# Folding channels c and c + 128 after the token transform, with the value path kept apart in three blocks of four

## The chip, the cores and the metric

The kernel runs on one core of a Trainium2 chip. The metric is the device time of one execution in microseconds (us). Every execution told of here was granted TensorE clock 0.999 to 1.0. PE is the tensor engine, DVE the vector engine, ACT the scalar engine, POOL GpSimd.

Differences under about 1 us between two programs are not read from their times. They are read, where possible, from the traces of the steady part, whose durations repeat within 0.02 us from batch to batch, apart from one or two chunks that differ by 0.1 to 0.3.

## The reference, cut to what matters

```python
X = np.fft.fft(x, axis=1)           # x: 8 batches x 3008 tokens x 256 channels
X = np.fft.fft(X, axis=2).real      # the mixing
g, val = X @ w_gate, X @ w_val      # 256 -> 1536
out = (gelu(g) * val) @ w_out       # 1536 -> 256
```

## The kernel before: the parts that matter

The token transform is split in two stages, and the channel transform stands between them. Stage 1 multiplies x with constants G and gives `A`; the channel stage multiplies `A` with cosines and sines `CS` and gives `Z`; the E, B and O packs (64-column matmuls on `Z`) give the even and odd parts of the mixed signal for half of the tokens. The feed-forward part ("layer 1", "layer 2") then makes token t and its mirror T - t from E + O and E - O.

```python
# stage 1, per group of 4 j: 2 x 4 matmuls of N=96, two evacuations on ACT
for cc in range(2):                       # channels 0..127, 128..255
    ...
    nc.tensor.matmul(ps[:, jj*96:(jj+1)*96], xt[:, j0+jj, cc*128:(cc+1)*128], G[:, j0+jj, :], ...)
# s1_ev: copies ps (128x384) to A[:, cc, ...], bf16

# channel stage, per pair of k2: 4 matmuls of N=256, one evacuation on DVE
for d in range(2):
    for cc in range(2):
        nc.tensor.matmul(ps[:, d*C:(d+1)*C], A[:, cc, k2+d, :], CS[:, cc, :], start=(cc==0), stop=(cc==1))
nc.vector.tensor_copy(Z[k2, k2+1], ps)

# layer 1 works on blocks fc of 128 hidden units, 12 per chunk, 3 chunks (512, 512, 481 tokens) per batch
def apart(ci, fc):
    return fc % 6 != 5 and (b, ci) != (0, 0)
# apart:     5 matmuls (gate E, O, M; value E, M), three DVE operations, product on POOL
# not apart: 6 matmuls (gate E, O, M; value E, O, M), two DVE products straight from PSUM
```

Work on the next batch (stage 1, channel stage, E/B/O) is slotted as "filler" between the blocks of the current batch: a batch has 36 slots, one per block. Batch 0's own transform is a head before the first block, and batch 1's filler is squeezed into the last 24 slots of batch 0. The head also makes all constants.

## Time and profile before

690.7 us is the median (690.18 to 691.16).

| | PE | DVE | POOL | ACT |
|---|---|---|---|---|
| busy, share of the span | 96% | 87% | 74% | 66% |
| busy in batch 3, of 81.01 us | 81.01 | 73.48 | 63.97 | 54.70 |

A busy PE is not a PE at its peak, so the chain of waits is read as well. This is the first line of the chain part of the page of the kernel before (shares of the span by engine):

```profile
PE 93%; POOL 3%; DVE 1%; ACT 1%; issue 1%; POOLq 0%; DVEq 0%; ACTq 0%
```

And this is the chain view of the same kernel for 275 to 356 us, nearly one batch of the steady part (shares of that stretch by engine, tile and line):

```profile
by line: PE ps_o L595 38.9%; PE ps_g L502 28.3%; PE ps_v L502 20.4%; PE ps_dft L402 6.5%; PE ps_dft L365 3.4%; PE ps_dft L427 0.8%; PE ps_dft L452 0.8%; PE ps_dft L440 0.8%
```

In the steady part nothing but PE is on the chain. L402 is the channel stage: 6.5% of it. The price of a matmul is its spacing, not its duration (durations overlap). The timeline of PE gives it: four matmuls of N=256 start at 301.58 and the next group at 302.02, so 110 ns each; two of N=512 are 216 ns apart.

```profile
301.15 0.38 PE L502 MATMUL ps_v<-EO_sb,WvE 128*128 128x512 bf16 x1
301.37 0.38 PE L502 MATMUL ps_v<-EO_sb,WvM 128*128 128x512 bf16 x1
301.58 0.60 PE L402 MATMUL ps_dft<-CS,A_sb 128*128 128x256 bf16 x4
302.02 1.04 PE L595 MATMUL ps_o<-Wo_sb,h_sb 128*128 128x256 bf16 x8
```

Finally, the groups (line, engine, operation, out<-in and shapes, count, busy us and mean ns, idle before) of what the change touches:

```profile
L412 DVE CAST Z_sb<-ps_dft 128x512 bf16<-128x512 f32 x88 | 60.1, 683 | 1.3 <-PE ps_dft L402 1.3
L402 PE MATMUL ps_dft<-CS,A_sb 128*128 128x256 bf16 x372 | 56.8, 274 | 0.3 <-DVE EO_sb L456 0.3
L379 ACT ACTIVATE A_sb<-ps_dft 128x384 bf16<-128x384 f32 x115 | 50.9, 503 | 0.6 <-PE ps_dft L365 0.5
L236 DVE CAST x_sb<-x_plain 94x1024 bf16<-94x1024 f32 x5 | 3.5, 695 | 0.6 <-DMA x_plain<-in_x_dram 0.6
```

### The profile page before, as it was taken

The page shows a single profiled execution, that of the slowest core. Times are in us where ns is not written, and L with a number is a line of the kernel's source. Part 1 is how long each engine was busy: PE and PEld are TensorE (multiplying, and loading weights), DVE is VectorE, ACT ScalarE, POOL GpSimd, SP SyncE. Part 2 cuts the span into 40 slices and gives each one's busy share as a digit, 9 for nine tenths or more (in the row PEclk, how much of TensorE's full clock was granted, in tenths as well). Part 3 has the DMA queues.
Part 4 walks back from the last instruction along what each step waited for, and adds up shares of the span by engine and source line. Part 5 has one row for each costly group of instructions (what it writes and reads, how often), then busy time and mean ns, then how long its engine had stood idle before and what let it go on. Part 6 is the DMA issues. An engine that isn't in the chain of part 4 may idle for free.

```text
span 689.5 us, 14359 instructions
## 1 busy us (share of the span) xinstructions
PE 664.8 (96%) x5290; PEld 455.7 (66%) x5290; DVE 603.0 (87%) x969; ACT 452.1 (66%) x892; POOL 507.0 (74%) x288
## 2 busy tenths in 40 slices
PE   2899999999999999999999999999999999999995
PEld 2556677766667666666667667676676666666664
DVE  7698899899988999889998899889998899999980
ACT  5689667756676656866678556776668666666650
POOL 8305777877887887788778868877886787798980
PEclk9999999999999999999999999999999999999999
DMA  8970611251114321161112621211112121221122
GB/s 234 208 151 17 129 39 38 50 116 40 43 35 90 75 47 35 44 120 45 39 40 47 117 47 33 46 37 38 40 39 47 28 47 32 47 47 43 38 51 62
DMA packets 36278, 43.44 MB, mean 63 GB/s; under 512 B 6668, under 2 KB 33292, under 8 KB 34700
## 3 DMA queue, kind: packets, MB, share of 16 engines
q1 hardware_dynamic: 32432, 30.47, 18.6%
q0 software_dynamic: 3184, 11.57, 9.4%
q8 instruction: 41, 0.67, 0.4%
q10 hardware_dynamic: 592, 0.49, 0.3%
q14 instruction: 29, 0.24, 0.1%
HBM read 29.43 MB, written 24.64 MB: 78 GB/s over the span
## 4 chain that ended last, share of the span: by engine, by line
PE 93%; POOL 3%; DVE 1%; ACT 1%; issue 1%; POOLq 0%; DVEq 0%; ACTq 0%
PE ps_o L595 36%; PE ps_g L502 26%; PE ps_v L502 19%; PE ps_dft L402 6%; PE ps_dft L365 3%; POOL h_sb L572 1%; PE ps_dft L452 1%; PE ps_dft L427 1%; PE ps_dft L440 1%; PE ps_v L332 0%; PE ps_g L332 0%; POOLq L758 0%; DVE out_sb L608 0%; DVE A_sb L381 0%; PE ps_v L402 0%
## 5 line engine op out<-in xcount | busy, mean ns | idle before, releaser
L572 POOL TENSOR_TENSOR h_sb<-gelu_sb,v_sb 128x1024 bf16<-128x1024 bf16 (+1 forms) x230 | 481.4, 2107 | 155.0 <-ACT gelu_sb L560 66.3
L595 PE MATMUL ps_o<-Wo_sb,h_sb 128*128 128x256 bf16 (+1 forms) x2304 | 299.2, 272 | 3.9 <-DVE out_sb L608 2.2
L517 ACT ACTIVATE gelu_sb<-ps_g 128x512 bf16<-128x512 f32 (+1 forms) x288 | 169.0, 587 | 150.9 <-PE ps_g L502 150.5
L595 PEld LDWEIGHTS <-h_sb 128*128 128x128 bf16 (+1 forms) x2304 | 220.5, 100 | 44.2 <-issue 5.0
L535 DVE SCALAR_TENSOR_TENSOR ve_sb<-EB_sb,w_97,ps_v 128x512 f32<-128x512 bf16 (+1 forms) x230 | 167.6, 729 | 22.6 <-PE ps_v L502 19.7
L560 ACT ACTIVATE gelu_sb<-ps_g 128x512 bf16<-128x512 f32 (+1 forms) x288 | 168.0, 584 | 2.8 <-PE ps_g L502 2.8
L539 DVE SCALAR_TENSOR_TENSOR v_sb<-ps_v,ve_sb 128x512 f32<-128x512 f32 (+1 forms) x230 | 155.4, 675 | 16.5 <-POOL h_sb L572 0.6
L541 DVE SCALAR_TENSOR_TENSOR v_sb<-ps_v,ve_sb 128x512 f32<-128x512 f32 (+1 forms) x230 | 153.8, 669 | 0.0
L502 PE MATMUL ps_g<-EO_sb,WgM 128*128 128x512 bf16 (+1 forms) x288 | 108.3, 376 | 0.0
L502 PE MATMUL ps_g<-EO_sb,WgO 128*128 128x512 bf16 (+1 forms) x288 | 108.2, 376 | 0.0
L502 PE MATMUL ps_v<-EO_sb,WvE 128*128 128x512 bf16 (+1 forms) x288 | 108.0, 375 | 0.0
L502 PE MATMUL ps_g<-EO_sb,WgE 128*128 128x512 bf16 (+1 forms) x288 | 108.0, 375 | 0.0
L502 PE MATMUL ps_v<-EO_sb,WvM 128*128 128x512 bf16 (+1 forms) x288 | 104.4, 376 | 0.4 <-DVE h_sb L547 0.2
L615 ACT ACTIVATE out_sb<-ps_o 128x512 f32<-128x512 f32 x92 | 55.0, 598 | 37.6 <-PE ps_o L595 36.0
L412 DVE CAST Z_sb<-ps_dft 128x512 bf16<-128x512 f32 x88 | 60.1, 683 | 1.3 <-PE ps_dft L402 1.3
L402 PE MATMUL ps_dft<-CS,A_sb 128*128 128x256 bf16 x372 | 56.8, 274 | 0.3 <-DVE EO_sb L456 0.3
L402 PEld LDWEIGHTS <-A_sb 128*128 128x128 bf16 x384 | 38.1, 100 | 24.3 <-issue 1.2
L575 DVE TENSOR_TENSOR h_sb<-gelu_sb,ps_v 128x512 bf16<-128x512 bf16 (+1 forms) x58 | 39.2, 677 | 15.0 <-ACT gelu_sb L560 13.0
L379 ACT ACTIVATE A_sb<-ps_dft 128x384 bf16<-128x384 f32 x115 | 50.9, 503 | 0.6 <-PE ps_dft L365 0.5
L365 PEld LDWEIGHTS <-x_sb 94*128 94x128 bf16 x512 | 30.6, 102 | 29.7 <-DVE x_sb L236 14.4
L502 PEld LDWEIGHTS <-WvE 128*128 128x128 bf16 x288 | 28.2, 98 | 32.2
L502 PEld LDWEIGHTS <-WvM 128*128 128x128 bf16 x288 | 28.2, 98 | 30.8 <-issue 0.8
(101 smaller groups left out, 393.5 us busy)
## 6 DMA issues: line engine op xcount, KB each, us to landing
out_dram<-out_sb SPq DMA_DIRECT2D x361, 64.0 KB, 2.0
x_sb<-in_x_dram POOLq DMA_DIRECT2D x14, 752.0 KB, 7.8
x_plain<-in_x_dram SPq DMA_DIRECT2D x4, 384.0 KB, 7.6
x_plain<-in_x_dram SPq DMA_DIRECT2D x2, 768.0 KB, 8.1
Wo_sb<-in_moe_w_out_dram POOLq DMA_DIRECT2D x2, 384.0 KB, 6.0
wg_hi<-in_moe_w_gate_dram SPq DMA_DIRECT2D x2, 256.0 KB, 3.8
wv_hi<-in_moe_w_val_dram SPq DMA_DIRECT2D x2, 256.0 KB
wg_lo<-in_moe_w_gate_dram SPq DMA_DIRECT2D x2, 256.0 KB, 4.8
```

The costliest lines, as they stand in the source:

```text
L365: nc.tensor.matmul(ps[:, jj * 96 : (jj + 1) * 96], xt[:, j0 + jj, cc * 128 : (cc + 1) * 128], G[:, j0 + jj, :], start=True, stop=True,)
L402: nc.tensor.matmul(ps[:, d * C : (d + 1) * C], A[:, cc, k2 + d, :], CS[:, cc, :], start=(cc == 0), stop=(cc == 1),)
L412: nc.vector.tensor_copy(_sub(Z, [[1, 2 * C]], k2 * C), ps)
L502: nc.tensor.matmul(ps[:, :n], W[nm, part][:, fs], src, start=start, stop=stop, **kw)
L517: nc.scalar.activation(gl[:, 0, :n], pg[:, :n], AF.Gelu)
L535: nc.vector.scalar_tensor_tensor(ve[:, :n], EB_bufs[b][:, c0 : c0 + n], w128[:, fc : fc + 1], pv[:, :n], op0=ALU.mult, op1=ALU.add)
L539: nc.vector.scalar_tensor_tensor(vv[:, 0, :n], po[:, :n], -0.5, ve[:, :n], op0=ALU.mult, op1=ALU.add)
L541: nc.vector.scalar_tensor_tensor(_sub(vv, [[-1, n]], TOK + n - 1), po[:, :n], 0.5, ve[:, :n], op0=ALU.mult, op1=ALU.add)
L560: nc.scalar.activation(dst, pg[:, :n], AF.Gelu)
L572: nc.gpsimd.tensor_tensor(st["h"][:, fc, :, :n], gl[:, :, :n], pv[:, :, :n], op=ALU.mult)
L595: nc.tensor.matmul(pso[:m, sign, :], st["h"][:, fc, sign, h0 : h0 + m], Wo_sb[:, fc, :], start=(fc == 0), stop=(fc == NFC - 1),)
L615: nc.scalar.activation(osb[:m], pso[:m], AF.Copy)
```

## The change

For even output channels the cosine and sine of channel c + 128 equal those of c, for odd ones they are their negatives. So the sum of channels c and c + 128 is enough for the even outputs, and their difference for the odd ones. The intent is to form both once, when stage 1 is evacuated, and to halve the columns of the channel stage's matmuls. DVE pays for the folds; Z's and O's evacuations move from DVE to ACT, and a further block in each chunk takes the six-matmul form, which costs DVE less and PE more.

```diff
 # stage 1, batches 1..7
-                s1_ev(j0, "AA")
+                up = up_tile()
+                nc.scalar.activation(up8, hi, AF.Copy)
+                for g, op in enumerate((ALU.add, ALU.subtract)):
+                    nc.vector.tensor_tensor(dst, lo, up8, op=op)      # dst in A[:, g]
 ...
             work.append(s1_pack(j0))
+            work.append(lambda: None)                                 # folds in every second filler place
 # channel stage
-                    for cc in range(2):  matmul(ps[:, d*C:(d+1)*C], A[:, cc, k2+d, :], CS[:, cc, :], ...)
+                    for g in range(2):   matmul(ps[:, o:o+128], A[:, g, k2+d, :], CS[:, g, :], start=True, stop=True)
-                    nc.vector.tensor_copy(Z, ps)
+                    nc.scalar.activation(Z, ps interleaved, AF.Copy)  # batch 0 alternates ACT and DVE, as before
 # O pack
-                nc.vector.tensor_copy(EO, ps)
+                nc.scalar.activation(EO, ps, AF.Copy)
 # value
-            return fc % 6 != 5 and (b, ci) != (0, 0)
+            return fc % 4 != 3 and (b, ci) != (0, 0)
 # head: batch 0's x
-    def cast_x(j0, nj, on_act=False):  one copy fp32 -> bf16 (DVE; j0 = 20 on ACT)
+    def fold_x(j0, nj):                add and subtract of two fp32 halves -> bf16, all on DVE
 # also: smaller constants CS without a POOL product, output buffers 3 -> 2
```

More of the change, by code (lines that the diff above doesn't have):

```diff
@@ L86 @@
     TPI = const_pool.tile([128, 2 * K1], BF16)
-    CS = const_pool.tile([128, 2, C], BF16)
+    CS = const_pool.tile([128, 2, 128], BF16)
     W = {}
@@ L113, in gelu_tile, with up_tile @@
         return work_pool.tile([128, 2, TOK], BF16, tag="gelu", bufs=4, name="gelu_sb")
+    def up_tile():
+        return work_pool.tile([128, 384], FP32, tag="up", bufs=2, name="up_sb")
     def ve_tile():
@@ L121, in osb_tile @@
     def osb_tile():
-        return work_pool.tile([128, 2, C], FP32, tag="osb", bufs=3, name="out_sb")
+        return work_pool.tile([128, 2, C], FP32, tag="osb", bufs=2, name="out_sb")
     def ps_g():
@@ L168 @@
     row_k = const_pool.tile([128, K2H], FP32)
-    row_c = const_pool.tile([128, C], FP32)
-    alt = const_pool.tile([128, C], BF16)
+    row_c = const_pool.tile([128, 128], FP32)
+    row_e = const_pool.tile([128, C], FP32)
     NPH = NJ * K2H
@@ L228, in g_sin, with fold_x @@
                 AF.Sin, scale=sc_g[:NP, h : h + 1])
-    def cast_x(j0, nj, on_act=False):
-        dst = _sub(x_tiles[0], [[1, nj * C]], j0 * C)
-        src = _sub(xs[j0 // 16], [[1, nj * C]], j0 % 16 * C, part_num=NP)
-        if on_act:
-            nc.scalar.activation(dst, src, AF.Copy)
-        else:
-            nc.vector.tensor_copy(dst, src)
+    def fold_x(j0, nj):
+        lo, hi = (_sub(xs[j0 // 16], [[C, nj], [1, 128]], j0 % 16 * C + i * 128, part_num=NP) for i in range(2))
+        for g, op in enumerate((ALU.add, ALU.subtract)):
+            nc.vector.tensor_tensor(_sub(x_tiles[0], [[C, nj], [1, 128]], j0 * C + g * 128), lo, hi, op=op)
     def spread(col, n):
@@ L250, in cs_phase @@
         nc.gpsimd.memset(col_m, MAGIC)
-        nc.gpsimd.iota(row_c[:, 0:129], pattern=[[1, 129]], base=0, channel_multiplier=0, **IOTA)
-        nc.gpsimd.iota(row_c[:, 129:256], pattern=[[1, 127]], base=1, channel_multiplier=0, **IOTA)
-        nc.gpsimd.memset(off[:, 0:129], 0.25)
-        nc.gpsimd.memset(off[:, 129:256], 0.0)
-        nc.gpsimd.memset(_sub(alt, [[2, C // 2]], 0), 1.0)
-        nc.gpsimd.memset(_sub(alt, [[2, C // 2]], 1), -1.0)
+        nc.gpsimd.iota(row_c, pattern=[[1, 128]], base=0, channel_multiplier=0, **IOTA)
+        nc.gpsimd.iota(row_e, pattern=[[1, 2], [0, 2], [2, 64]], base=0, channel_multiplier=0, **IOTA)
+        nc.gpsimd.memset(row_e[:, 64:65], 128.0)
+        nc.gpsimd.memset(_sub(off, [[128, 2], [1, 64]], 0), 0.25)
+        nc.gpsimd.memset(_sub(off, [[128, 2], [1, 64]], 64), 0.0)
+        nc.gpsimd.memset(off[:, 64:65], 0.25)
         nc.gpsimd.tensor_scalar(col_q, col_p, 1.0 / C, None, op0=ALU.mult)
-        nc.gpsimd.tensor_tensor(fp, row_c, spread(col_q, C), op=ALU.mult)
+        nc.gpsimd.tensor_tensor(fp, row_e, spread(col_q, C), op=ALU.mult)
         nc.gpsimd.tensor_tensor(fp, fp, off, op=ALU.add)
@@ L262, in cs_sin @@
     def cs_sin():
-        nc.scalar.activation(CS[:, 0, :], dc, AF.Sin, scale=-TWO_PI)
-        nc.gpsimd.tensor_tensor(CS[:, 1, :], CS[:, 0, :], alt, op=ALU.mult)
+        nc.scalar.activation(_sub(CS, [[1, C]], 0), dc, AF.Sin, scale=-TWO_PI)
     def t_phase():
@@ L385, in run @@
                 s1_mm(j0)
-                s1_ev(j0, "AA")
+                lo, hi = (_sub(st.pop((j0, cc)), [[1, 2 * K2H], [96, 4], [2 * K2H, 2]], 0) for cc in range(2))
+                up = up_tile()
+                up8 = _sub(up, [[8, 2 * K2H], [2, 4], [1, 2]], 0)
+                nc.scalar.activation(up8, hi, AF.Copy)
+                for g, op in enumerate((ALU.add, ALU.subtract)):
+                    dst = _sub(st["A"], [[64, 2 * K2H], [2, 4], [1, 2]], g * K2H * 128 + j0 * 2)
+                    nc.vector.tensor_tensor(dst, lo, up8, op=op)
             return run
@@ L400, in run @@
                 for d in range(2):
-                    for cc in range(2):
+                    for g in range(2):
+                        o = g * C + d * 128
                         nc.tensor.matmul(
-                            ps[:, d * C : (d + 1) * C],
-                            A[:, cc, k2 + d, :],
-                            CS[:, cc, :],
-                            start=(cc == 0),
-                            stop=(cc == 1),
-                        )
+                            ps[:, o : o + 128], A[:, g, k2 + d, :], CS[:, g, :], start=True, stop=True)
+                dst = _sub(Z, [[1, 2 * C]], k2 * C)
+                src = _sub(ps, [[64, 4], [1, 64], [C, 2]], 0)
                 if b == 0 and k2 // 2 % 2 == 1:
-                    nc.scalar.activation(_sub(Z, [[1, 2 * C]], k2 * C), ps, AF.Copy)
+                    nc.vector.tensor_copy(dst, src)
                 else:
-                    nc.vector.tensor_copy(_sub(Z, [[1, 2 * C]], k2 * C), ps)
+                    nc.scalar.activation(dst, src, AF.Copy)
             return run
@@ L455, in run @@
                 off = HALF + chunk_off[gi]
-                nc.vector.tensor_copy(_sub(EO, [[1, n]], off), ps[:, :n])
+                nc.scalar.activation(_sub(EO, [[1, n]], off), ps[:, :n], AF.Copy)
                 nc.scalar.activation(
@@ L646 @@
         g_sin(0, 8)
-        cast_x(0, 4)
+        fold_x(0, 4)
         s1_mm(0)
@@ L650 @@
         g_sin(8, 8)
-        cast_x(4, 4)
+        fold_x(4, 4)
         s1_mm(4)
@@ L657 @@
         cs_sin()
-        cast_x(8, 8)
+        fold_x(8, 8)
         s1_mm(8)
@@ L663 @@
         t_sin()
-        cast_x(16, 4)
-        cast_x(20, 4, True)
+        fold_x(16, 4)
+        fold_x(20, 4)
         s1_mm(16)
@@ L669 @@
         s1_ev(20, "VA")
-        cast_x(24, 4)
+        fold_x(24, 4)
         s1_mm(24)
         s1_ev(24, "VA")
-        cast_x(28, 4)
+        fold_x(28, 4)
         s1_mm(28)
```

## The prediction

> **What bounds the kernel now.** The tensor engine. The chain of waits is 93% PE; the windows show PE busy 70.0 of 70 us in every stretch from 120 to 610 us; one batch takes 81.05 us (the same L2 block in the chain: 268.27 to 349.28). Matmul spacing in the timeline is about 216 ns for N=512, 205 for 481, 109 for 256, 43 for 96, 28 for 64. So a batch is 39.3 (layer 1, 186 matmuls) + 31.4 (layer 2) + 2.7 (stage 1) + 5.2 (channel stage, 48 of N=256) + 2.1 (E, B, O) = 80.7 us: PE hardly waits. DVE is next: 63 of 70 us. ACT is 68%, POOL 79%.
>
> **What the change removes, adds, moves** (estimates from these spacings; back to back, a 512-wide DVE operation costs 0.60 us, the three value operations 1.85).
> - PE: the channel stage's matmuls go from N=256 to 128, estimated 56 ns (N=64 with its own weights ran at 28, so weight loads don't bind): 48 x 53 ns = 2.5 us less per batch. In 23 chunks one more block has six instead of five layer-1 matmuls: 0.64 us more per batch. Net 1.9 per batch, some 14.5 us in all if nothing else binds.
> - DVE: Z and O evacuations leave (9 us a batch), three blocks lose 1.85 and gain 1.2; 16 folds of 384 elements arrive, about 0.48 each (a 384-wide cast took 0.56, less overlap). Per batch 71 falls to 68 us.
> - ACT: 8 copies less, 15 more: 72%. POOL: 23 products of 2.1 us less; not critical.
>
> **How much is on the critical path.** All of PE's 1.9 us, but DVE's load moves within the batch: folds fall in the first 16 of 36 slots. There four slots cost DVE 3 x 1.85 + 1.2 + 4 x 0.48 = 8.7 us, and PE also 8.7 (21 x 216 + 32 x 109 + two stage-1 packs of 0.34). With three value buffers DVE cannot lag far, so PE should lose about 0.7 us per batch waiting for ps_v. In batch 0 the fillers are squeezed into 24 slots: 2 to 3 us lost.
>
> In the head DVE's casts (0.69 us per four j) become an add and a subtract of fp32 SBUF tensors, about 1.25 us, and one cast moves from ACT to DVE. The Trainium skill, "VectorE: DVE Perf Modes", perf-mode tier table, gives fp32 copies 2x and fp32 tensor_tensor 1x; the trace's cast (1024 elements, 0.69 us) agrees. "SBUF — State Buffer", Who interferes with whom, says two SBUF inputs contend with GpSimd reads: rd took 0.85 us beside POOL and 0.56 elsewhere. The head grows about 3.5 us; cheaper channel packs give 1.5 back: +2.
>
> Sum: 691 - 14.5 + 2 + 2.5 + 5 (stalls) = 686, less about 1 in the tail; I say 684.5.
>
> **Prediction.** 684.5 us, 8 in 10 between 677.5 and 691. Faster by over 2% (under 677): 0.08; within 2%: 0.88; slower: 0.04.
>
> **What would show it right or wrong.** Channel matmuls spaced near 56 ns, their share of the chain falling from 6.0% to 3%; a batch period of 79.5 to 80.5 us; folds of about 0.56 us in the groups; DVE near 97% in the first 16 slots of a batch and 80% in the rest (windows), with ps_v or ps_dft matmuls waiting for DVE in the first part; first channel pack at 24.5 us instead of 21.3; POOL 64%.
>
> **What would make it wrong.** Folds much dearer than casts, or in-order ACT delaying Z so that PE waits (slower); slack absorbing the folds without stalls and the head hidden behind loads (about 677).

## The result

The changed kernel took 683.12 us (682.33 to 684.08, 4 runs) against 690.74 us (690.18 to 691.16, 4 runs). The ratio is 0.9891, with a 95% interval of 0.9872 to 0.9910. A ratio is always the mean time of one kernel's fast runs over that of the other's of the same rounds, so not quite the ratio of the medians. The saving is 7.6 us, 1.1%.

The chain for 274 to 353 us of the changed kernel, nearly one batch of its steady part:

```profile
by line: PE ps_o L603 39.9%; PE ps_g L510 28.3%; PE ps_v L510 22.0%; PE ps_dft L365 3.4%; PE ps_dft L413 3.4%; PE ps_dft L460 0.9%; PE ps_dft L435 0.9%; PE ps_dft L448 0.9%; issue 0.5%
```

It is still PE alone, and the channel stage (now L413) fell from 6.5% to 3.4%. The timeline of PE shows four of its matmuls in 0.23 us, 57 ns each:

```profile
98.17 0.39 PE L413 MATMUL ps_dft<-CS,A_sb 128*128 128x128 bf16 x4
98.40 1.04 PE L603 MATMUL ps_o<-Wo_sb,h_sb 128*128 128x256 bf16 x8
```

The groups that answer to those of before; L393 is the folds, which take 0.55 us each, and L420 Z's evacuation, now on ACT:

```profile
L393 DVE TENSOR_TENSOR A_sb<-ps_dft,up_sb 128x384 bf16<-128x384 f32 x112 | 57.4, 549 | 0.0
L420 ACT ACTIVATE Z_sb<-ps_dft 128x512 bf16<-128x512 f32 x88 | 52.5, 601 | 0.2 <-PE ps_dft L413 0.2
L413 PE MATMUL ps_dft<-CS,A_sb 128*128 128x128 bf16 x372 | 37.7, 222 | 0.3 <-DVE WgO L335 0.3
```

**Where the time went.** The first gelu of a block is a clock that both kernels have in common. The table gives the moments in both traces at which it starts, and the growing difference.

| moment (us) | before | after | difference | so the stretch in front of it gained (-) or lost (+) |
|---|---|---|---|---|
| first gelu of batch 0 | 29.64 | 32.72 | +3.08 | head +3.08 |
| first gelu of batch 1 | 112.75 | 115.95 | +3.20 | batch 0: +0.12 (its chunks: -0.95, -2.09, +3.16) |
| first gelu of batch 7 | 598.88 | 590.73 | -8.15 | six batches: -11.35, or -1.89 each |
| last block's first gelu | 667.51 | 659.89 | -7.62 | batch 7: +0.53 |
| end of the span | 689.5 | 681.9 | -7.6 | tail: 0 |

The steady batches gain just what PE's work loses: the 48 channel matmuls a batch are 53 ns cheaper (2.5 us), the three added ones cost 0.64, so 1.9. Two things eat into it: the head, and batch 0. There the PE work (weight loads counted in the trace times the spacings, an estimate good to some 0.3 us) of the second and third chunk is 53.7 us, and they take 57.8. Before, the work was 56.5 us and the time 56.7.

DVE was expected to be full while the folds run, and it is. The windows view gives per stretch the length and then busy us (and instructions) of PE, PE's weight loads, DVE, ACT and POOL, the clock and DMA. These are slots 0 to 15 and 16 to 35 of batch 3 in the kernel before,

```profile
274.83:310.32 35.49, 35.49 (x288) 24.66 (x286) 31.37 (x49) 25.34 (x53) 27.35 (x16) 1.00 0.40 82
310.32:355.84 45.52, 45.52 (x374) 31.48 (x373) 42.10 (x69) 29.36 (x57) 36.61 (x18) 1.00 0.18 40
```

and in the changed kernel:

```profile
274.10:308.03 33.93, 33.72 (x266) 23.16 (x267) 33.64 (x59) 22.36 (x45) 23.57 (x12) 1.00 0.22 46
308.03:353.18 45.15, 44.99 (x395) 31.32 (x397) 36.13 (x58) 36.82 (x73) 34.09 (x18) 1.00 0.33 71
```

DVE is busy 33.64 of 33.93 us (99%) in the fold phase and 80% after it; before it was 88% and 92%. Yet the batch takes 79.08 us, its PE work. So DVE is full and costs nothing, which the prediction had not expected. The experiments ask whether that is real slack or an edge, and what the head and batch 0 pay for.

### The profile page after: what moved, and what is told of

Its sections match the earlier page's. It is cut to its first block, busy times and chain, and to the rows that moved or that the text cites. A ratio compares the mean times of both kernels' runs of the same rounds, so it can differ in the third digit from the quotient of the medians.

```text
span 681.9 us, 14383 instructions
## 1 busy us (share of the span) xinstructions
PE 652.0 (96%) x5257; PEld 443.7 (65%) x5313; DVE 580.4 (85%) x958; ACT 484.7 (71%) x943; POOL 459.9 (67%) x264
## 4 chain that ended last, share of the span: by engine, by line
PE 81%; DVE 2%; ACT 2%; issue 1%; POOL 1%; DMA 1%; SPq 0%; ACTq 0%; DVEq 0%
PE ps_o L603 33%; PE ps_g L510 23%; PE ps_v L510 18%; PE ps_dft L413 3%; PE ps_dft L365 2%; POOL h_sb L580 1%; DMA out_dram<-out_sb 1%; DVE v_sb L547 1%; PE ps_dft L448 1%; PE ps_dft L460 1%; PE ps_dft L435 1%; DVE v_sb L549 0%; ACT gelu_sb L568 0%; DVE ve_sb L543 0%; ACT out_sb L623 0%
## 5 line engine op out<-in xcount | busy, mean ns | idle before, releaser
L580 POOL TENSOR_TENSOR h_sb<-gelu_sb,v_sb 128x1024 bf16<-128x1024 bf16 (+1 forms) x207 | 433.4, 2104 | 193.0 <-ACT gelu_sb L568 122.5
L603 PE MATMUL ps_o<-Wo_sb,h_sb 128*128 128x256 bf16 (+1 forms) x2304 | 308.9, 272 | 4.2 <-DVE out_sb L616 2.1
L543 DVE SCALAR_TENSOR_TENSOR ve_sb<-EB_sb,w,ps_v 128x512 f32<-128x512 bf16 (+1 forms) x207 | 150.5, 732 | 46.0 <-PE ps_v L510 45.6
L547 DVE SCALAR_TENSOR_TENSOR v_sb<-ps_v,ve_sb 128x512 f32<-128x512 f32 (+1 forms) x207 | 140.0, 676 | 12.9 <-PE ps_v L510 0.5
L549 DVE SCALAR_TENSOR_TENSOR v_sb<-ps_v,ve_sb 128x512 f32<-128x512 f32 (+1 forms) x207 | 138.7, 670 | 0.0
L510 PE MATMUL ps_g<-EO_sb,WgO 128*128 128x512 bf16 (+1 forms) x235 | 88.4, 376 | 0.1
L555 DVE TENSOR_TENSOR h_sb<-gelu_sb,ps_v 128x512 bf16<-128x512 bf16 (+1 forms) x81 | 54.5, 674 | 9.6 <-PE ps_v L510 7.6
L583 DVE TENSOR_TENSOR h_sb<-gelu_sb,ps_v 128x512 bf16<-128x512 bf16 (+1 forms) x81 | 54.7, 676 | 7.6 <-PE ps_v L510 3.7
L393 DVE TENSOR_TENSOR A_sb<-ps_dft,up_sb 128x384 bf16<-128x384 f32 x112 | 57.4, 549 | 0.0
L420 ACT ACTIVATE Z_sb<-ps_dft 128x512 bf16<-128x512 f32 x88 | 52.5, 601 | 0.2 <-PE ps_dft L413 0.2
L510 PEld LDWEIGHTS <-WgM 128*128 128x128 bf16 x288 | 28.2, 98 | 29.5
```

The costliest lines, as they stand in the source:

```text
L393: nc.vector.tensor_tensor(dst, lo, up8, op=op)
L510: nc.tensor.matmul(ps[:, :n], W[nm, part][:, fs], src, start=start, stop=stop, **kw)
L543: nc.vector.scalar_tensor_tensor(ve[:, :n], EB_bufs[b][:, c0 : c0 + n], w128[:, fc : fc + 1], pv[:, :n], op0=ALU.mult, op1=ALU.add)
L547: nc.vector.scalar_tensor_tensor(vv[:, 0, :n], po[:, :n], -0.5, ve[:, :n], op0=ALU.mult, op1=ALU.add)
L549: nc.vector.scalar_tensor_tensor(_sub(vv, [[-1, n]], TOK + n - 1), po[:, :n], 0.5, ve[:, :n], op0=ALU.mult, op1=ALU.add)
L555: nc.vector.tensor_tensor(st["h"][:, fc, 0, :n], gl[:, 0, :n], pv[:, :n], op=ALU.mult)
```

## The experiments

Below, "the changed kernel" is the reference (683.12 us) unless said otherwise.

### The two parts of the change, each alone

Fold alone: the changed kernel with one line undone.

```diff
-            return fc % 4 != 3 and (b, ci) != (0, 0)
+            return fc % 6 != 5 and (b, ci) != (0, 0)
```

> The fold without the second part (value apart in five blocks of six, as before). Theory P (PE alone sets the pace, DVE queue absorbs the folds without loss): PE loses the 23 added matmuls of about 0.21 us, so 683.1 - 4.9 = about 678 us, batch period 78.4 us. Theory D (DVE is already full in the first 16 of 36 slots, 98 to 100% busy in the changed kernel, so more value work there stalls PE): four slots cost DVE 3.33 x 1.85 + 0.67 x 1.2 + 4 x 0.48 = 8.9 us against 8.6 on PE, so 1 to 1.5 us per batch are lost there: 683 to 687 us, period 79.5 to 80.

Second part alone: the kernel before with the opposite edit of the same line.

> The kernel before with only the second part (value apart in three blocks of four). If PE sets the pace: 23 matmuls of about 0.21 us more, 690.7 + 4.9 = 695.6 us, period 81.7 us. If DVE or POOL held the kernel before anywhere in the steady state, their relief (DVE 0.65 us per block, POOL 2.1 us per block) gives something back: under 693 us.

Measured, medians in us:

| | value apart in 5 of 6 | in 3 of 4 | effect of the second part |
|---|---|---|---|
| no fold | 690.7 to 691.1 (the kernel before) | 698.81 (698.71 to 699.06) | +7.7 |
| fold | 685.91 (683.67 to 686.35) | 683.12 | -2.8 |

The second part costs 7.7 us without the fold, and gains 2.8 with it. Theory D holds in kind: DVE stands at an edge in the fold phase. Its own figures were too large, though (1 to 1.5 us lost per batch, a period of 79.5 to 80). With the fold alone a batch takes 79.14 us (batch 3), though PE has three matmuls fewer than in the changed kernel and would need 78.4; 0.7 us a batch are lost. In the steady batches the second part therefore only breaks even: its 0.64 us of matmuls buy back those 0.7 us (79.08 against 79.14). Of the 1.8 us between the two profiled executions, 1.2 lie in batch 0 and 1.0 behind the last block's first gelu; the last batch before that gives 0.5 back. The chain of the fold-alone kernel from 275 to 355 us shows where the 0.7 us go (the view cuts the line off at its end):

```profile
by line: PE ps_o L603 27.9%; PE ps_g L510 19.3%; PE ps_v L510 15.4%; issue 6.7%; DVE v_sb L549 6.5%; DVE ve_sb L543 4.3%; DVE A_sb L393 4.1%; POOL h_sb L580 4.1%; DVE v_sb L547 3.8%; PE ps_dft L413 3.3%; PE ps_dft L365 1.3%; PE ps_dft L460 
```

DVE's value operations and folds (L393) are now on the chain, with POOL's product of gate and value behind them. In the order of time, a part of the chain from 299 to 305 us (start, length, what):

```profile
298.56 0.69 DVE v_sb L549
...
299.39 1.10 POOL h_sb L580
300.49 0.99 issue
301.48 2.16 POOL h_sb L580
303.64 0.05 issue
303.69 0.50 PE ps_o L603 x3
```

So a late DVE reaches PE here mostly by another way than the prediction's wait for ps_v. It makes the value late, POOL's product later, and the second layer's matmul (ps_o) waits for that product: PE stood still from about 303.41 to 303.69. This gap of 0.28 us is the largest of three that matmul spacing shows in batch 3 (places where only the record of a matmul is missing left out). At 307.67 a ps_o matmul waits 0.15 us for ACT's evacuation of a ps_o buffer. At 327.09, after the fold phase, a ps_v matmul waits 0.16 us for DVE's product, which is the kind of wait that the prediction named. Together they are 0.58 of the 0.7 us, and batch 4 shows the same three. POOL has more products in this run too (30 a batch instead of 27), but it is busy only 25.12 of the 34.14 us of batch 3's fold phase, and the phase-wise run below has as many products a batch without a loss (12 against 13 of them in the fold phase); so its lateness is most likely handed on, not made there.

The second part alone cost more than expected: the expectation was 695.6 us, and a batch took 82.10 us instead of 81.02, +1.08, where three matmuls explain 0.64. Most of the rest lies in the third chunk (+0.55, of which 0.20 is its one added matmul). The trace shows what PE waits for: in batch 3 an E matmul at 353.33 (0.16 us) for DVE's evacuation of Z and a channel matmul at 344.27 (0.18) for DVE's evacuation of O; in the second chunk another E matmul, at 317.07 (0.13), again for Z. These three gaps, 0.47 us together, explain the 0.44. Why DVE comes late there, with less value work than before, is not settled.

### The head

x of batch 0 is cast as before, not folded. Its output is wrong, which doesn't matter for the time.

```diff
-        for g, op in enumerate((ALU.add, ALU.subtract)):
-            nc.vector.tensor_tensor(x_tile half g, lo, hi, op=op)
+        (nc.scalar.activation(dst, src, AF.Copy) if j0 == 20 else nc.vector.tensor_copy(dst, src))
```

> Changed kernel, but x of batch 0 is cast as before instead of folded (wrong values in batch 0 on purpose). If the DVE folds make the head 3.1 us longer: first gelu at about 29.7 us instead of 32.7 and 680.0 us in all. Rival: the head is longer through the new constants or the first channel evacuation waiting for ACT's table load: first gelu stays above 31.5 and the time above 682.

Measured 679.80 us (678.81 to 680.42), first gelu at 29.37. The folds in the head, with the one cast that moved from ACT to DVE, cost 3.3 us. DVE's timeline near the end of the head shows it in the kernel before,

```profile
17.69 0.68 DVE L236 CAST x_sb<-x_plain 94x1024 bf16<-94x1024 f32 x1
18.97 0.56 DVE L381 CAST A_sb<-ps_g 128x384 bf16<-128x384 f32 x1 [0.59 <-PE ps_g L365]
```

and in the changed kernel, where the same four j take an add and a subtract:

```profile
20.33 1.28 DVE L237 TENSOR_TENSOR x_sb<-x_plain 94x512 bf16<-94x512 f32 x2
21.61 0.56 DVE L381 CAST A_sb<-ps_g 128x384 bf16<-128x384 f32 x1
22.08 1.28 DVE L237 TENSOR_TENSOR x_sb<-x_plain 94x512 bf16<-94x512 f32 x2
```

It is 1.28 us instead of 0.68, for the same 1024 elements per partition. This agrees with the table that the prediction took from the Trainium skill, "VectorE: DVE Perf Modes" (section "The perf-mode tier table"). The port that DVE and GpSimd share shows as well. The skill's "SBUF — State Buffer" (section "Who interferes with whom") says that a DVE instruction with two SBUF inputs contends with GpSimd instructions that read SBUF. Here is the pair of 1024-wide folds, and what POOL did beside it:

```profile
12.80 2.81 DVE L237 TENSOR_TENSOR x_sb<-x_plain 94x1024 bf16<-94x1024 f32 x2
...
13.26 1.26 POOL L247 TENSOR_TENSOR small<-small,col_m 128x128 f32<-128x128 f32 x1
14.60 1.26 POOL L248 TENSOR_TENSOR small<-small,col_m 128x128 f32<-128x128 f32 x1
```

The first of these two POOL operations took 0.40 us before the change and the second 0.73; both take 1.26 beside the folds.

### Batch 0: folds, Z, or crowding

Four runs. First, batch 1's stage 1, which runs inside batch 0, without folds (wrong in batch 1 on purpose):

```diff
                 s1_mm(j0)
+                if b == 1:
+                    s1_ev(j0, "AA")
+                    return
```

> Changed kernel, but batch 1's stage 1 (which runs inside batch 0's 24 slots) is evacuated by ACT as before, without folding on DVE (wrong values in batch 1 on purpose). Theory F (the folds overload DVE in batch 0, as predicted): the 4.1 us that batch 0 loses to waits come back, about 679 us, batch 0's last chunk near 29 us instead of 31.8. Rival Z (Z evacuations on ACT, squeezed into batch 0's last chunk, make PE wait): last chunk stays above 31 us and the time at 682 to 683.

Second, the folds kept, and the second chunk of batch 0 all in the six-matmul form (correct):

```diff
-            return fc % 4 != 3 and (b, ci) != (0, 0)
+            return fc % 4 != 3 and (b, ci) not in ((0, 0), (0, 1))
```

> Changed kernel, but the second chunk of batch 0 has all twelve blocks with six matmuls: 9 x 0.216 = 1.9 us more on PE, 9 x 0.65 = 5.9 us less on DVE just where the folds are crowded. If DVE's load there is the cause of the 4.1 us, 2.8 us come back as in the run without folds: batch 0's second and last chunk together 57 us instead of 57.8, 682.3 us. If DVE is not the cause: 59.7 us together, 685 us.

Third, batch 1's Z on DVE (correct):

```diff
-                if b == 0 and k2 // 2 % 2 == 1:
+                if b == 1 or b == 0 and k2 // 2 % 2 == 1:
                     nc.vector.tensor_copy(dst, src)
```

> Changed kernel, but batch 1's Z evacuations (inside batch 0) go to DVE instead of ACT, as before the change; results correct. Taking the folds away gave back 2.8 of the 4.1 us that batch 0 loses. If the other 1.3 us are PE waiting for Z behind the gelus on ACT: batch 0's last chunk falls from 31.8 to about 30.5 us, 681.8 us. If DVE's total load in batch 0 is what counts: last chunk at 33 us or more (12 evacuations of 0.6 us added to DVE), 685 us or more.

Fourth, batch 1's filler spread over 28 slots (correct):

```diff
-            first_slot = NFC
+            first_slot = 8
```

> Changed kernel; batch 1's transform work is spread over 28 slots of batch 0 (from slot 8) instead of 24 (from slot 12). If the crowding of folds in batch 0 makes it lose 4 us to waits: about 2.5 us come back, 680.5 us, and batch 0's last chunk falls from 31.8 to about 29 us while its first chunk grows by at most 1 us. If the crowding is not the cause: the first chunk grows by what the last one gains, 682.5 to 684.

| | time, us | batch 0's second + third chunk, us |
|---|---|---|
| changed kernel | 683.12 | 25.96 + 31.81 = 57.77 |
| no folds in batch 1 | 680.87 (680.73 to 681.01) | 26.07 + 29.06 = 55.13 |
| second chunk all six-matmul | 682.51 (682.22 to 682.73) | 27.64 + 29.06 = 56.70 |
| Z of batch 1 on DVE | 683.62 (683.54 to 684.51) | 25.96 + 31.50 = 57.46 |
| spread over 28 slots | 682.12 (681.89 to 682.72) | 28.74 + 29.01 = 57.75 |

The windows of the second chunk of batch 0 (columns as above), in the changed kernel,

```profile
58.18:84.14 25.96, 25.55 (x197) 16.52 (x199) 25.67 (x45) 17.95 (x36) 15.70 (x9) 1.00 0.14 32
```

and with that chunk in the six-matmul form:

```profile
58.21:85.85 27.64, 27.64 (x220) 18.20 (x219) 22.56 (x40) 19.38 (x37) 1.03 (x2) 1.00 0.30 61
```

DVE goes from 25.67 of 25.96 us to 22.56 of 27.64. PE was given nine matmuls more (1.9 us), and the two chunks together became 1.1 us shorter: PE waits about 3 us less. Taking the folds away gains 2.6 us. Both say the same: DVE's load in that chunk makes PE wait for about 2.8 of the 4.1 us. Much of the loss shows up later than its cause, in the third chunk: PE does there what it left undone in the second (24.6 us of work in 26.0), and it waits there as well (about 29.1 us of work in 31.8).

The way from DVE to PE is seen in part only. This is the chain of the changed kernel for 58 to 116 us (it can be followed back only to about 80, and the view cuts the line off),

```profile
by line: PE ps_o L603 19.2%; PE ps_g L510 12.7%; PE ps_v L510 9.5%; ACT Z_sb L420 3.4%; ACT out_sb L623 2.8%; ACT gelu_sb L525 2.8%; ACT gelu_sb L568 2.6%; PE ps_dft L413 2.3%; issue 1.5%; PE ps_dft L365 1.4%; DVE h_sb L583 1.2%; PE ps_dft 
```

and, with the second chunk in the six-matmul form, for 58 to 115 us:

```profile
by line: PE ps_o L603 33.4%; PE ps_g L510 25.5%; PE ps_v L510 22.3%; PE ps_dft L365 4.5%; PE ps_dft L413 4.2%; ACT gelu_sb L525 2.0%; ACT Z_sb L420 1.7%; ACT gelu_sb L568 1.6%; PE ps_dft L460 1.2%; PE ps_dft L448 1.2%; PE ps_dft L435 1.2%; 
```

The last thing that PE waits for is mostly ACT: its gelus and evacuations are 11.6% of the first line and 5.3% of the second. The two runs show that DVE's load is behind this; the steps between DVE and ACT are not shown.

Moving Z from ACT to DVE brings nothing: it changes the two chunks by 0.3 us, and the next chunk gets 0.7 longer. My expectation for the rival there (third chunk at 33 us or more) missed as well. This does not clear ACT. In that run's third chunk PE waits for ACT's evacuations of E and O and for gelus instead (gaps of up to 0.4 us). And in the run without folds and in the six-matmul run alike, the third chunk keeps three gaps in which PE waits for ACT, 0.39 and 0.31 us for Z and 0.20 for O: 0.9 us of what is left. Crowding in slots is not the whole story either: over 28 slots the second chunk grows by 2.78 and the third shrinks by 2.80. The run is 1.0 us faster in the median, and its first gelu is 1.6 us earlier, which the edit doesn't explain. Why ACT is late in the remaining 1.3 us of batch 0, and why spreading doesn't help, stay open.

### Versions that might beat both

If DVE is at its limit only while folds run, the six-matmul blocks are wanted only there:

```diff
-            return fc % 4 != 3 and (b, ci) != (0, 0)
+            if (b, ci) == (0, 0): return False
+            if b == 0: return fc % 4 != 3
+            if b == B - 1: return fc % 4 != 3 if ci == 2 else fc % 6 != 5
+            return fc not in ((3, 7, 11), (3, 11), (11,))[ci]
```

> Changed kernel; in batches 1 to 6 the six-matmul blocks stay at 3, 7, 11 in the first chunk (where the folds run), and are only 3, 11 in the second and 11 in the third chunk; the last batch has every sixth block, its last chunk every fourth; 20 six-matmul blocks fewer. If DVE is the limit only while folds run: chunk 2 saves 0.22 us and chunk 3 0.41 us per batch, 683.1 - 4.3 = about 679 us, first chunk unchanged at 25.7 us. If DVE or POOL is full everywhere: no change, 682.5 to 684.

Measured 680.46 us (679.98 to 681.13). In the steady batches the first chunk takes 25.63 us (-0.06), the second 26.79 (-0.16), the third 26.03 (-0.41). A batch is 78.45 us, and DVE is at 99% in the fold phase and 86% after it:

```profile
272.56:306.43 33.87, 33.87 (x268) 23.09 (x266) 33.59 (x59) 22.34 (x45) 23.55 (x12) 1.00 0.22 46
306.43:351.01 44.58, 44.58 (x395) 31.09 (x394) 38.50 (x61) 36.70 (x72) 40.31 (x21) 1.00 0.34 72
```

This is the period that the fold alone should have had. It also clears POOL: it makes 30 products a batch, as with the fold alone, is busy 40.31 of 44.58 us (90%) after the fold phase, and PE doesn't wait.

Batch 0 unfolded, with its channel stage as pairs of accumulating N=128 matmuls and a negated copy of the odd constants:

```diff
 # x of batch 0 cast as in the section on the head (cut)
+        nc.scalar.activation(CSn, dc[:, 128:256], AF.Sin, scale=TWO_PI)
+        if b == 0:
+            for cc in range(2):
+                matmul(ps[:, o:o+128], A[:, cc, k2+d, :], CSn if (g, cc) == (1, 1) else CS[:, g, :], start=(cc==0), stop=(cc==1))
```

> Changed kernel; batch 0 alone is not folded: x cast as before, and the channel stage of batch 0 adds up both channel halves by four accumulating pairs of N=128 matmuls, with a negated copy of the odd constants (correct results). The head gets its 3.1 us back (first gelu near 29.7), the 12 channel packs of batch 0 cost PE 0.22 us more each, some of it behind other waits: 681 to 682 us. If channel packs in the head bind on PE, the gain is under 1 us.

Measured 681.29 us (680.26 to 682.25), correct. The first gelu is at 29.22 us (-3.5); batch 0 gives 1.0 of it back (its chunks: +1.87, +0.16, -1.05).

All three edits together (phase-wise pattern, unfolded batch 0, filler over 28 slots), and then two mixes with batch 1's Z on DVE:

> The three edits together. If the causes are separate (DVE in the fold phase, crowding in batch 0, head), the gains add: 683.1 - 4.3 - 2.5 - 1.5 = about 675 us. If batch 0's loss only moves between head and chunks, 677 to 679.

> Phase-wise value blocks, unfolded batch 0, and batch 1's Z on DVE; no spreading. The three-edit kernel with spreading took 678.45 us. Phase (-2.7) and head (-1.8) add to 678.6; if Z on DVE helps in batch 0, 677.5; if it hurts, 680 or more.

> As the three-edit kernel with spreading (678.45 us), plus batch 1's Z on DVE. If ACT's Z held PE in batch 0: 677.2 us; if DVE's load counts: 680 us or more.

Measured 678.45 us (678.27 to 678.67), 678.07 (677.76 to 679.18) and 679.11 (678.50 to 680.00). The gains of the three edits, measured one by one (2.7, 1.0, 1.8), would add to 677.6 us; the three together fall 0.8 short, and stay 3.4 above the 675 that I had expected, since batch 0 keeps its loss (58.5 us for its second and third chunk); this is the other branch of that expectation (677 to 679). The two mixes fall between the branches of theirs, so they say nothing of Z. The best kernel is the phase-wise pattern with the unfolded batch 0, Z of batch 1 on DVE and no spreading: 0.9821 of the kernel before (0.9806 to 0.9836). It and the three-edit kernel (0.9824) are not told apart. Both beat the changed kernel by some 5 us.

## Why the prediction was right or wrong

The time was right: 684.5 us was predicted, 683.12 measured. Part of that is two errors that cancel.

- **PE's gain, 1.9 us per batch.** Right: 1.89 measured, channel matmuls at 57 ns against 56 predicted, their share of the chain halved.
- **PE bounds the kernel before.** Right for the steady part (chain).
- **DVE near 97% in the first 16 slots, 80% in the rest.** Right: 99% and 80%.
- **"PE should lose about 0.7 us per batch waiting for ps_v".** Wrong, and this is the largest mis-sized term: 5 us were booked for all batches and 0 were lost. I had found equal loads, 8.7 us per four slots on both engines, and taken equality as a stall. The runs show that equal loads fitted. Only with 0.65 us more DVE work for each of three blocks a batch (the fold alone) did 0.7 us a batch appear, and then mostly not through ps_v: of 0.58 us of gaps in batch 3, POOL's late product makes 0.28, ACT's evacuation of layer 2 0.15, and ps_v waiting for DVE 0.16. The second part of the change is what keeps it just inside the edge.
- **Batch 0, 2 to 3 us.** The mechanism held: DVE's load where the folds run costs about 2.8 us there. The whole loss to waits in batch 0's last two chunks was larger (4.1). In 0.9 us of the rest PE waits for ACT's evacuations of Z and O; why they are late is open. The reason that I gave, fillers squeezed into 24 slots, is not supported: 28 slots did no better.
- **Head, +2 us.** Mechanism right (folds instead of casts), size off: +3.1. The first channel pack came at 23.97 us, 2.6 later than before (24.5 and 3.2 predicted). But the 1.5 us that cheaper channel packs were to give back did not come: from the first pack to the first gelu it took 8.7 us, and 8.3 before.
- **Tail, -1.** It was 0.
- **POOL 64%.** It is 67%: a slip in subtraction, as 507 busy us less 23 products of 2.1 is 459 of 682. (The batch of 81.05 us is another: 349.28 less 268.27 is 81.01.)

In sum, predicted: -14.5 (PE's work) + 2 (head) + 2.5 (batch 0) + 5 (stalls) - 1 (tail) = -6. Measured: -14.8 + 3.1 + 4.1 + 0 + 0 = -7.6, where -14.8 is -11.35 of six batches, +0.53 of the last, and an estimated -4.0 for batch 0 (its time grew by 0.12, of which 4.1 are put down to waits; about 2.8 of the -4.0 are less PE work in its last two chunks, and 0.95 is its shorter first chunk). Head and batch 0 were taken too low by 2.7 us, the stalls too high by 5.

## What to carry to other kernels

Take relief and load by phase, not by the average: the same line of code (more matmuls to spare DVE) cost 7.7 us where DVE had room and gained 2.8 where it was full (in batch 0 and at the end; the steady batches broke even), and applying it only in the full phase was better still. An engine that is 99% busy beside an equally busy PE need not cost anything; test with a little more load whether it stands at an edge, and look in the chain for the way by which its lateness reaches PE. Check the one-time parts (head and first batch) separately, since they took back about a third of what the steady part gained.

## What the Trainium skill lacked or had wrong

- "TensorE: Matmul & The Clock Gate", section "Back-to-back issue gap", says that a stream of weight loads and matmuls sustains about 81 ns per matmul at N=128 and 131 ns at N=512, and that its formula N/2.4 + 2.5 ns for isolated matmuls doesn't hold in a real kernel. Here every matmul has its own weight load, and the spacing is 57 ns at N=128, 110 at N=256 and 216 at N=512: close to the formula, not to the sustained figures.
- "SBUF — State Buffer", section "Who interferes with whom", says that the side which comes second blocks until the other's instruction is over, but not what two streams of instructions cost each other. Here both sides took longer: the pair of 1024-wide folds 2.81 us (four 512-wide ones, as many elements, took 2.48 from 16.99 us on), and POOL's 128-wide operations 1.26 beside them, against 0.40 and 0.73 in the kernel before. Each of the two ended about 0.25 us after the fold beside it (14.52 and 15.86 against 14.27 and 15.61), which would fit that rule; no run isolates it.
- "ScalarE: Activation LUTs" doesn't say what a stepped read from PSUM costs. ACT's evacuation of Z, which takes pairs that lie 1 KiB apart in a bank, took 601 ns on average, against 585 for the contiguous one of the same 512 elements in the kernel before (5 of them): at most a few per cent.
